# Wv and Wo on GpSimd's DMA queue, and a new order of the preamble, in a two-layer segment-recurrent transformer on one NeuronCore

## Chip, cores and metric

The kernel runs on one core of one Trainium2 chip. The metric is device time in microseconds (us) of one execution, lower is better. Three runs of the kernel before gave 1550.52, 1552.66 and 1554.28 us; the median, 1552.66 us, is the time before. The profiled execution has a span of 1549.6 us with a granted TensorE clock of 0.999.

## What is computed

```
def A(x, mem0, Wq, Wk, Wv, Wo):            # S=2048, Dm=448, H=16, Dh=256, seg=32, M=8
    mem = mem0
    for s in range(64):
        h = concat([mem, x[segment s]])    # 40 rows
        q, k, v = h Wq, h Wk, h Wv         # per head
        p = softmax(mask(q k^T * Dh**-0.5))
        o = sum over heads of (p v) Wo
        mem = o[:8]; outs.append(o[8:])    # the memory rows feed the next segment
def B(x): return (relu(x W_gate) * (x W_up)) W_down     # F=1792
x = x + A(layernorm(x)); x = x + B(layernorm(x))
x = x + A(layernorm(x)); x = x + B(layernorm(x))        # the same weights again
```

Everything is bfloat16 outside PSUM. The 64 segments of one attention layer are a recurrence through `mem`.

## The kernel before

**Folding.** The kernel never forms q, k and v. For each head it forms M = Wk Wq^T and B = Wv Wo once, in a preamble (448x448 each), and keeps them in SBUF for the whole run: `M_sb`/`MT_sb` and `B_sb`/`BT_sb`, where the `T` tiles hold the tail of 64 of the 448 rows. A step then computes G from M and the segment's transposed rows (`GPhase`), the scores S from G, the softmax, the values VO = h B (`Values`, lines 373 to 413), and their weighted sum.

**Steps.** Line 921 runs 70 steps. The first layer's chain C1 takes steps 0 to 63, the second layer's chain C2 runs six steps behind. A step with one chain is `single`, one with two is `dual`. The feed-forward blocks are filled into the steps.

**Preamble (lines 892 to 918).** The weights come in eight parts for Wv and Wo (two heads each) and four parts for Wk and Wq (four heads each):

- `load_vo(j)` (line 174) issues three plain loads: 384 rows of Wv (384 KB), its last 64 rows (64 KB), and 448 KB of Wo. Wv goes to one of two fixed tiles `wvn`, so part j+2 can only be loaded when `turn_B(j)` has read part j. Wo has two buffers, freed by `make_B(j)`.
- `load_kq(i)` (line 171) issues two transposing loads (`load_T`, line 164), each 896 KB: Wk and Wq arrive with the head dimension on the partitions. Each has two buffers, so part i+2 waits for `make_M(i)`.
- `turn_B(j)` transposes a Wv part on TensorE in 16 instructions; `make_B(j)` multiplies in 32; `make_M(i)` multiplies in 32. Their PSUM banks are copied out by ScalarE and VectorE in turn (`copy_out`), those of `make_B(7)` by ScalarE alone.
- `prep_stats`, `prep_rows`, `prep_pe` normalise and transpose 128 rows of x for chain C1. The normalisation takes a reciprocal square root from two GpSimd instructions (lines 253 and 254).
- `first_G[0].quarter(k)` computes a quarter of step 0's G; it needs M from `make_M(k)`.

**What sets the order.** All these loads are issued on SyncE's queue (SP), one after the other. `in_order` (line 117) chains the TensorE instructions, and the loads, in the order in which they are written; a scheduler places the other instructions. The written order of the preamble is: loads of vo 0, vo 1, kq 0; B 0 and B 1; M 0; first x rows; B 2, B 3; M 1; B 4, B 5; quarters 0 and 1; M 2; quarter 2; M 3; quarter 3. Step 0 then has `turn_B(6)`, `turn_B(7)`, `make_B(6)` in its hook `mid` (ahead of the scores) and `make_B(7)` in its hook `soft` (behind the scores, while the softmax runs), and after that the values: `vm` for the memory and a part of the rows, `v` for the others. `part(x, True)` is the tail (with `BT_sb`), `part(x, False)` the body; x = 0 takes the heads of the even B parts, x = 1 those of the odd ones (`place`, line 40).

**GpSimd before.** It clears `memTp`, `mbs`, `PXM`, `PTs` and `maskf` at the start, and issues no loads.

Of the kernel before, what the change touches and what calls it, by code (L numbers as in the profile page):

```python
# [9 lines left out]
BF = mybir.dt.bfloat16  # L10
# [41 lines left out]
def build_kernel(ctx, tc, A_x, A_mem0, A_Wq, A_Wk, A_Wv, A_Wo, B_W_gate, B_W_up, B_W_down, out,  # L52
# [9 lines left out]
    glob = ctx.enter_context(tc.tile_pool(name="glob", bufs=1))  # L62
    R = min(6, ntiles)
    x_ring = glob.tile([P, R, DM], BF)
    nc.sync.dma_start(x_ring[:, 0:2, :], x_dram[0:256].rearrange("(t p) d -> p t d", p=P))

    def xsl(t):
        return x_ring[:, t % R, :]
# [19 lines left out]
    nc.scalar.dma_start(mem_in[:, DM:DMP], mem0[:, 384:448])  # L88
    memTp = []
    for i in range(2):  # L90
        mt = glob.tile([P, NSL, SEG], BF, name=f"memTp{i}")
        nc.gpsimd.memset(mt[:], 0.0)
        memTp.append(mt)
    mbs = []
    for i in range(3):
        m = glob.tile([P, DMP], BF, name=f"mb{i}")
        nc.gpsimd.memset(m[:], 0.0)
        mbs.append(m)
    xns = [glob.tile([P, DMP], BF, name=f"xn{i}") for i in range(2)]
    xds = [glob.tile([P, NCH, 2, 64], BF, name=f"xd{i}") for i in range(2)]  # L100
    n_xn = [0, 0]
    mhalf = glob.tile([P, 1], F32)
    nc.gpsimd.memset(mhalf[:], -0.5)
    p_ln = ctx.enter_context(tc.tile_pool(name="p_ln", bufs=2))

    psum = ctx.enter_context(tc.tile_pool(name="psum", bufs=8, space=bass.MemoryType.PSUM))
# [10 lines left out]
    def in_order(op):  # L117

        eng = op.ins.engine
        if eng in last_of:  # L120
            tc.add_manual_dep(op.ins, last_of[eng],
                              mybir.DependencyInfo(mybir.DependencyClass.NoSync, mybir.DependencyReason.DATA),
                              reason="in_order")
        last_of[eng] = op.ins.name
# [9 lines left out]
    p_pp = ctx.enter_context(tc.tile_pool(name="p_pp", bufs=1))  # L134
    PXM = []
    for i in range(2):
        pp = [p_pp.tile([P, H, SEG], BF, name=f"P{n}{i}") for n in "xm"]
        for q in pp:
            nc.gpsimd.memset(q[:], 0.0)
        PXM.append(pp)  # L140
    PTs = [p_pp.tile([P, 8, P], BF, name=f"PT{i}") for i in range(2)]
    for q in PTs:
        nc.gpsimd.memset(q[:], 0.0)

    bpre = ExitStack()
    bp = bpre.enter_context(tc.tile_pool(name="bpre", bufs=2))
    wvn = [bp.tile([P, NSL, 512], BF, name=f"wvn{i}", bufs=1) for i in range(2)]
    for w in wvn:
        nc.vector.memset(w[HI, 3], 0.0)
    maskf = bp.tile([P, L], F32, bufs=1)  # L150
    nc.gpsimd.memset(maskf[:], 0.0)
    nc.gpsimd.affine_select(
# [4 lines left out]
    nc.vector.memset(maskb[:], 0.0)  # L157
    for half in HALVES:
        nc.vector.tensor_copy(maskb[half], maskf[LO].unsqueeze(1).to_broadcast([64, 8, L]))

    srcs = {n: w.rearrange("d h e -> d (h e)") for n, w in (("k", A_Wk), ("q", A_Wq), ("v", A_Wv))}
    WoF = A_Wo.rearrange("h (t p) d -> p (h t) d", p=P)

    def load_T(n, i):
        t = bp.tile([P, 8, DM], BF, tag=f"w{n}", name=f"w{n}")
        in_order(nc.sync.dma_start_transpose(t[:], srcs[n][:, 1024 * i:1024 * (i + 1)]))  # L166
        return t

    kq, vo = {}, {}

    def load_kq(i):
        kq[i] = load_T("k", i), load_T("q", i)

    def load_vo(j):

        w, cols = wvn[j % 2], slice(512 * j, 512 * j + 512)
        in_order(nc.sync.dma_start(w[:, 0:3, :], srcs["v"][0:384, cols].rearrange("(c p) e -> p c e", p=P)))
        in_order(nc.sync.dma_start(w[LO, 3, :], srcs["v"][384:448, cols]))
        wo = bp.tile([P, 4, DM], BF, tag="wo", name="wo")
        in_order(nc.sync.dma_start(wo[:], WoF[:, 4 * j:4 * (j + 1), :]))  # L180
        vo[j] = w, wo

    flip = [0]

# [18 lines left out]
    def make_M(i):  # L203

        wk, wq = kq.pop(i)
        for hh in range(4):
            o = 896 * ((4 * i + hh) // 2)
            for mt in range(3):
                ps = psum.tile([P, 512], F32, tag="ps")
                product(ps[:, 0:DM], wk, wq, hh, 128 * mt, 128)  # L210
                store_M(M_sb[:, mt, o:o + 896], hh % 2, ps[:, 0:DM])
        for e in range(2):
            ps = psum.tile([P, 512], F32, tag="ps")
            for side in range(2):
                product(ps[64 * side:64 * side + 64, 0:DM], wk, wq, 2 * side + e, 384, 64)
            store_M(MT_sb[:, 896 * i:896 * i + 896], e, ps[:, 0:DM])
# [3 lines left out]
    def turn_B(j):  # L220

        wn = vo[j][0]
        wv = wv_T[j] = bp.tile([P, 4, DM], BF, tag="wv", name="wv")
        for a in range(2):
            tp = psum.tile([P, 2, 512], BF, tag="ps", name="tp")
            for b in range(2):
                for dc in range(NSL):
                    transpose(tp[:, b, 128 * dc:128 * dc + 128],
                              wn[:, dc, 128 * (2 * a + b):128 * (2 * a + b) + 128], ident[:])
            copy_out(wv[:, 2 * a:2 * a + 2, :], tp[:, :, 0:DM])  # L230

    def make_B(j):

        wv, wo = wv_T.pop(j), vo.pop(j)[1]
        for hh in range(2):
            for mt in range(3):
                ps = psum.tile([P, 512], F32, tag="ps")
                product(ps[:, 0:DM], wv, wo, hh, 128 * mt, 128)
                copy_out(B_sb[:, mt, place(2 * j + hh), :], ps[:, 0:DM], j == 7)
        ps = psum.tile([P, 512], F32, tag="ps")  # L240
        for e, half in enumerate(HALVES):
            product(ps[half, 0:DM], wv, wo, e, 384, 64)
        copy_out(BT_sb[:, place(2 * j), :], ps[:, 0:DM], j == 7)
# [320 lines left out]
    def single(g, c, inG, mid, soft, before, late, end, last):  # L564
# [67 lines left out]

        alone = g + 1 < LAG if c is C1 else g + 1 < nsteps and (g + 1 - c.lag) % 4 != 0
        soft()
        if not g:
            vm.both(True)
        vm.both(False)
        if odd:
            vox = prev_vom[0]
            v = ahead[g + 1] = x_values(g + 1) if alone else None  # L640
        else:
            v = ahead.pop(g, None)
            if v is None:
                v = x_values(g)
                v.part(0, False)
                v.part(0, True)
            v.part(1, True)
            vox = v.dst
        prev_vom[0] = VOm
        before()  # L650
# [231 lines left out]
    def none():  # L882
        pass

    def make_two(j):
        turn_B(j)
        turn_B(j + 1)
        for i in (j, j + 1):
            make_B(i)
            load_vo(i + 2)  # L890

    load_vo(0)
    load_vo(1)
    load_kq(0)
    make_two(0)
    load_kq(1)
    make_M(0)
    tps0 = transposed(mem_in, MEM)
    nc.vector.tensor_copy(mem0T[:], tps0[:, :, 0:MEM])
    set_mem0(C1)  # L900
# [2 lines left out]
        prep_rows(C1, t)  # L903
        prep_pe(C1, t)
    make_two(2)
    load_kq(2)
    make_M(1)
    load_kq(3)
    make_two(4)
    if R > 2:  # L910
        in_order(nc.sync.dma_start(x_ring[:, 2:R, :], x_dram[256:R * 128].rearrange("(t p) d -> p t d", p=P)))
    first_G.append(GPhase(0))
    for i in range(2):
        first_G[0].quarter(i)
    make_M(2)
    first_G[0].quarter(2)
    make_M(3)
# [3 lines left out]
    for g in range(nsteps):  # L921
        gb, r = divmod(g, 4)
        if g == LAG:
            set_mem0(C2)
        inG = mid = soft = before = late = end = last = none
        if g == 0:
            def mid():
                turn_B(6)
                turn_B(7)
                make_B(6)  # L930

            def soft():
                make_B(7)
                late_pools()
        elif r == 0:
            def inG():
                fill(0, 1)

            def mid():
                fill(0, 2)  # L940

            def end():
                fill(0, 1)

            def last():
                fill(0, 1)
        elif r == 1:
            def inG():
                prep_stats(C1, gb + 2, recent["G"])

            def mid():
                prep_rows(C1, gb + 2, recent["G"])
                fill(0, 2)

            def before():
                fill(0, 3)
                prep_stats(C2, gb - 1)
                prep_rows(C2, gb - 1)

            def end():  # L960
                prep_pe(C1, gb + 2)
                fill(1, 1)
                prep_pe(C2, gb - 1)

            def last():
                fill(1, 1)
        elif r == 2:
            def inG():
                fill(1, 1)

            def mid():
                fill(1, 1)

            def end():
                fill(1, 1)

            def last():
                fill(1, 1)
        else:
            def mid():  # L980
                fill(1, 1)
                load_x()

            def before():
                fill(1, 1)

            def end():
                fill(1, 1)

            def last():  # L990
                fill(1, 1)
        step(g, inG, mid, soft, before, late, end, last)
        for c in (C1, C2):
            t, j = divmod(g - c.lag, 4)
            if j == 3 and 0 <= t < ntiles:
                f = FFN(c, t)
                f.norm()
                if c is C2 and recent["two"] and g + 1 < nseg and t:
                    f.rows(recent["sum"])
                ffn_q[c.cid].extend(f.pieces())  # L1000
# [54 lines left out]
```

## Time and profile before

| | |
|---|---|
| time, median of 3 | 1552.66 us (1550.52 to 1554.28) |
| profiled span | 1549.6 us |
| TensorE (PE) busy | 1515.6 us, 98% |
| VectorE (DVE), ScalarE (ACT), GpSimd (POOL) busy | 910.5, 625.7, 148.2 us |
| first TensorE instruction | 4.66 us |
| `make_M(0)` begins | 17.39 us |
| `make_M(3)` begins | 57.69 us |
| step 0's first instruction (mask into S) | 65.47 us |
| step 1's first instruction | 83.50 us |

Where PE is busy 98% of the span, only PE's idle time, or PE work that falls away, can shorten it. A line of the timeline gives the start, the length from the first start to the last end, engine, operation, tiles and count, and in brackets the idle time before it and what ended it. SPq is SyncE's sequencer issuing a DMA: its length is the issue, not the transfer. Rows of windows give for each stretch the busy time of each engine, and at the end the granted clock, the DMA engines' busy share (over 1 where packets overlap) and GB/s.

### The profile page before, as it was taken

Reading aid. Unit: us, or ns where it says so; the run is one execution under the profiler, and the core shown is the slowest. Engines: PE = TensorE matmul, PEld = TensorE weight load, DVE = VectorE, ACT = ScalarE, POOL = GpSimd, SP = SyncE. Lnnn points to the kernel's source line nnn. Section 1 sums busy time; section 2 is a strip of 40 time slices with the busy share of each in tenths; the row PEclk is TensorE's granted clock in tenths of the full one; section 3 lists DMA queues with packets and bytes.
Section 4 is the critical chain, followed back from the end, with each engine's and each line's share of the span. In section 5 each row is a group of like instructions: output and inputs, shape, how many; then the busy total and the mean of one; then the engine's idle time right before and its main releaser. Section 6 shows DMA issues by size and latency. Waiting matters only on the chain.

```text
span 1549.6 us, 82294 instructions
## 1 busy us (share of the span) xinstructions
PE 1515.6 (98%) x38579; PEld 1141.7 (74%) x38579; DVE 910.5 (59%) x2085; ACT 625.7 (40%) x1459; POOL 148.2 (10%) x384
## 2 busy tenths in 40 slices
PE   7999999999999999999999999999999999999998
PEld 4566777778777777777778777877777787777775
DVE  5535466665656566556656566565656665656543
ACT  5634344434344343434434343434434343444333
POOL 2001011010101001010001101010100100001000
PEclk9999999999999999999999999999999999999999
DMA  9731000010000000000000101001000000000000
GB/s 238 161 91 44 5 11 15 10 21 12 10 15 16 17 12 19 12 21 6 14 17 12 21 10 21 12 12 14 16 17 12 17 12 14 10 7 14 5 8 9
DMA packets 83636, 39.20 MB, mean 25 GB/s; under 512 B 65752, under 2 KB 82400, under 8 KB 83296
## 3 DMA queue, kind: packets, MB, share of 16 engines
q1 hardware_dynamic: 83264, 33.94, 10.3%
q8 instruction: 301, 4.93, 1.3%
q14 instruction: 39, 0.32, 0.1%
q10 hardware_dynamic: 32, 0.01, 0.0%
HBM read 14.00 MB, written 1.84 MB: 10 GB/s over the span
## 4 chain that ended last, share of the span: by engine, by line
PE 92%; DMA 2%; DVE 2%; SPq 2%; ACT 1%; issue 0%; POOL 0%; POOLq 0%; ACTq 0%
PE gps L127 30%; PE vps L127 28%; PE gate L127 11%; PE AT_ps L127 7%; PE dps L127 6%; PE S_ps L127 5%; PE PT_ps L130 2%; SPq L166 1%; DMA wq<-in_A_Wq_dram 1%; DMA xnT_1184<-xd_91 1%; PE up L127 1%; PE ps L127 1%; PE mps L127 1%; PE tps L130 0%; DVE G L474 0%
## 5 line engine op out<-in xcount | busy, mean ns | idle before, releaser
L127 PE MATMUL gps<-hTr,M_sb 128*128 128x80 bf16 (+1 forms) x11760 | 414.7, 198 | 0.0
L127 PEld LDWEIGHTS <-M_sb 128*128 128x128 bf16 x11760 | 405.3, 99 | 4.4
L474 DVE CAST G<-gps 128x480 bf16<-128x480 f32 (+2 forms) x327 | 194.0, 611 | 222.1 <-PE gps L127 221.4
L474 ACT CAST G<-gps 128x480 bf16<-128x480 f32 (+2 forms) x327 | 165.6, 525 | 350.7 <-PE gps L127 350.7
L127 PEld LDWEIGHTS <-hTr 128*32 128x32 bf16 (+3 forms) x8000 | 177.3, 93 | 142.2 <-issue 42.2
L127 PE MATMUL vps<-B_sb,hTr 128*32 128x448 bf16 x4464 | 234.2, 353 | 0.0
L127 PEld LDWEIGHTS <-Wgu 64*128 64x128 bf16 x6272 | 181.0, 94 | 21.8 <-issue 13.0
L407 ACT CAST VOm<-vps 128x448 bf16<-128x448 f32 x251 | 121.5, 529 | 124.5 <-PE vps L127 124.4
L407 ACT CAST vox<-vps 128x448 bf16<-128x448 f32 x186 | 96.1, 533 | 93.4 <-PE vps L127 89.6
L337 DVE SCALAR_TENSOR_TENSOR hh<-gate,ut 128x256 bf16<-128x256 f32 x224 | 94.7, 423 | 66.4 <-ACT ut L336 66.3
L407 DVE CAST vox<-vps 128x448 bf16<-128x448 f32 x186 | 112.8, 619 | 27.4 <-PE vps L127 25.0
L336 ACT CAST ut<-up 128x256 bf16<-128x256 f32 x224 | 83.8, 374 | 64.8 <-PE up L127 64.8
L127 PE MATMUL up<-xnT_1183,Wgu 64*128 64x128 bf16 x1568 | 104.0, 216 | 0.0
L127 PE MATMUL gate<-xnT_1183,Wgu 64*128 64x128 bf16 x1568 | 103.9, 216 | 0.0
L127 PE MATMUL gate<-xnT_1184,Wgu 64*128 64x128 bf16 x1568 | 99.3, 216 | 2.9 <-DMA xnT_1184<-xd_91 1.8
L127 PE MATMUL up<-xnT_1184,Wgu 64*128 64x128 bf16 x1568 | 99.3, 216 | 0.0
L127 PE MATMUL gps<-hTr,MT_sb 64*128 64x80 bf16 (+1 forms) x3920 | 91.5, 195 | 4.4 <-ACT hTr L693 2.1
L127 PE MATMUL dps<-Wd,hh 128*128 128x448 bf16 x448 | 92.7, 353 | 0.0
L127 PE MATMUL S_ps<-G,hTr 128*8 128x320 bf16 (+3 forms) x2048 | 86.2, 299 | 2.1 <-DVE G L474 1.7
L127 PEld LDWEIGHTS <-MT_sb 64*128 64x128 bf16 x3920 | 76.4, 96 | 15.2 <-issue 7.6
L127 PE MATMUL vps<-B_sb,memTp_80 128*32 128x448 bf16 x1680 | 85.7, 352 | 0.0
L127 PE MATMUL vps<-B_sb,memTp_78 128*32 128x448 bf16 x1680 | 85.7, 352 | 0.0
(163 smaller groups left out, 1607.0 us busy)
## 6 DMA issues: line engine op xcount, KB each, us to landing
wo<-in_A_Wo_dram SPq DMA_DIRECT2D x8, 448.0 KB, 5.4
out_dram<-x_ring SPq DMA_DIRECT2D x16, 112.0 KB, 1.7
Wgu<-in_B_W_gate_dram SPq DMA_DIRECT2D x7, 224.0 KB, 3.5
Wgu<-in_B_W_up_dram SPq DMA_DIRECT2D x7, 224.0 KB, 3.4
Wd<-in_B_W_down_dram SPq DMA_DIRECT2D x7, 224.0 KB, 2.7
wvn_124<-in_A_Wv_dram SPq DMA_DIRECT2D x4, 384.0 KB, 3.7
wvn_125<-in_A_Wv_dram SPq DMA_DIRECT2D x4, 384.0 KB, 6.2
x_ring<-in_A_x_dram SPq DMA_DIRECT2D x10, 112.0 KB, 2.8
```

What stands on the lines that cost most here:

```text
L127: in_order(nc.tensor.matmul(*a, **k))
L130: in_order(nc.tensor.transpose(*a))
L166: in_order(nc.sync.dma_start_transpose(t[:], srcs[n][:, 1024 * i:1024 * (i + 1)]))
L336: recent["ut"] = nc.scalar.copy(ut[:], gu[1][:])
L337: recent["hh"] = nc.vector.scalar_tensor_tensor(out=self.hh[:, f:f + 2, :], in0=gu[0][:], scalar=0.0, in1=ut[:], op0=ALU.max, op1=ALU.mult)
L407: op = self.evac[2 * x + e](self.dst[:, 2 * e + x, :], self.ps[x][e][:, 0:DM])
L474: op = (cp_a, cp_v)[self.side](gp.G[:, self.side, self.t0:self.t0 + self.n, gp.c0:gp.c1, :], self.ps[:, 0:self.n * gp.NP].rearrange("p (m ...
```

## The change

It moves the loads of Wv and Wo to GpSimd's queue, so that Wk and Wq have SyncE's queue to themselves with x; keeps the first transposing load back until the first Wo part has landed; moves the clears on GpSimd behind the first six loads; and gives the preamble and step 0 another order. The core of the diff:

```diff
-    nc.sync.dma_start(x_ring[:, 0:2, :], x_dram[0:256].rearrange("(t p) d -> p t d", p=P))
...
-        nc.gpsimd.memset(mt[:], 0.0)
...
-        nc.gpsimd.memset(m[:], 0.0)
...
-        for q in pp:
-            nc.gpsimd.memset(q[:], 0.0)
...
-    for q in PTs:
-        nc.gpsimd.memset(q[:], 0.0)
...
+    def load_T(n, i):
+        t = bp.tile([P, 8, DM], BF, tag=f"w{n}", name=f"w{n}")
+        dma = nc.sync.dma_start_transpose(t[:], srcs[n][:, 1024 * i:1024 * (i + 1)])
+        if not i and n == "k":
+            tc.add_manual_dep(dma.ins, first_wo[0].ins.name,
+                              mybir.DependencyInfo(mybir.DependencyClass.Sync, mybir.DependencyReason.DATA),
+                              reason="first_wo")
+        in_order(dma)
+        return t
...
+        in_order(nc.gpsimd.dma_start(w[:, 0:3, :], srcs["v"][0:384, cols].rearrange("(c p) e -> p c e", p=P)))
+        in_order(nc.gpsimd.dma_start(w[LO, 3, :], srcs["v"][384:448, cols]))
+        wo = bp.tile([P, 4, DM], BF, tag="wo", name="wo")
+        dma = nc.gpsimd.dma_start(wo[:], WoF[:, 4 * j:4 * (j + 1), :])
+        in_order(dma)
+        first_wo.append(dma)
...
+    load_vo(0)
+    load_vo(1)
+
+    nc.gpsimd.memset(mhalf[:], -0.5)
...
+    for q in memTp + mbs + PXM[0] + PXM[1] + PTs:
+        nc.gpsimd.memset(q[:], 0.0)
...
-    def make_B(j):
+    def make_B(j, between=None):
...
         for hh in range(2):
+            if hh and between:
+                between()
...
-        if not g:
-            vm.both(True)
-        vm.both(False)
+        if g:
+            vm.both(False)
+        else:
+            v = ahead[0] = x_values(0)
+            for x in range(2):
+                vm.part(x, True)
+                v.part(x, True)
+                vm.part(x, False)
+                if not x:
+                    v.part(0, False)
...
-            v.part(1, True)
+            if g:
+                v.part(1, True)
...
     def make_two(j):
-        turn_B(j)
-        turn_B(j + 1)
         for i in (j, j + 1):
-            make_B(i)
-            load_vo(i + 2)
-
-    load_vo(0)
-    load_vo(1)
+            make_B(i, (lambda: turn_B(j + 1)) if i == j else None)
+            if i + 2 < 8:
+                load_vo(i + 2)
+
+    first_G.append(GPhase(0))
     load_kq(0)
+    load_first_x(0, 2)
+    load_kq(1)
+    turn_B(0)
     make_two(0)
-    load_kq(1)
     make_M(0)
+    load_kq(2)
+    turn_B(2)
     tps0 = transposed(mem_in, MEM)
...
     make_two(2)
-    load_kq(2)
     make_M(1)
     load_kq(3)
+    if R > 2:
+        load_first_x(2, R)
+    turn_B(4)
+    first_G[0].quarter(0)
     make_two(4)
-    if R > 2:
-        in_order(nc.sync.dma_start(x_ring[:, 2:R, :], x_dram[256:R * 128].rearrange("(t p) d -> p t d", p=P)))
-    first_G.append(GPhase(0))
-    for i in range(2):
-        first_G[0].quarter(i)
+    first_G[0].quarter(1)
     make_M(2)
...
             def mid():
                 turn_B(6)
-                turn_B(7)
-                make_B(6)
 
             def soft():
-                make_B(7)
+                make_two(6)
                 late_pools()
```

`load_first_x` is a new helper that issues the old x load on SyncE's queue, chained by `in_order`.

More of the change, by code (lines that the diff above doesn't have):

```diff
@@ L90, in build_kernel @@
     for i in range(2):
-        mt = glob.tile([P, NSL, SEG], BF, name=f"memTp{i}")
-        nc.gpsimd.memset(mt[:], 0.0)
-        memTp.append(mt)
+        memTp.append(glob.tile([P, NSL, SEG], BF, name=f"memTp{i}"))
     mbs = []
     for i in range(3):
-        m = glob.tile([P, DMP], BF, name=f"mb{i}")
-        nc.gpsimd.memset(m[:], 0.0)
-        mbs.append(m)
+        mbs.append(glob.tile([P, DMP], BF, name=f"mb{i}"))
     xns = [glob.tile([P, DMP], BF, name=f"xn{i}") for i in range(2)]
@@ L102, in build_kernel @@
     mhalf = glob.tile([P, 1], F32)
-    nc.gpsimd.memset(mhalf[:], -0.5)
     p_ln = ctx.enter_context(tc.tile_pool(name="p_ln", bufs=2))
@@ L136, in build_kernel @@
     for i in range(2):
-        pp = [p_pp.tile([P, H, SEG], BF, name=f"P{n}{i}") for n in "xm"]
-        for q in pp:
-            nc.gpsimd.memset(q[:], 0.0)
-        PXM.append(pp)
+        PXM.append([p_pp.tile([P, H, SEG], BF, name=f"P{n}{i}") for n in "xm"])
     PTs = [p_pp.tile([P, 8, P], BF, name=f"PT{i}") for i in range(2)]
-    for q in PTs:
-        nc.gpsimd.memset(q[:], 0.0)
     bpre = ExitStack()
@@ L149, in build_kernel, with load_kq, load_vo @@
         nc.vector.memset(w[HI, 3], 0.0)
+    srcs = {n: w.rearrange("d h e -> d (h e)") for n, w in (("k", A_Wk), ("q", A_Wq), ("v", A_Wv))}
+    WoF = A_Wo.rearrange("h (t p) d -> p (h t) d", p=P)
+    def load_T(n, i):
[7 more added lines that the diff above has]
+        return t
+    kq, vo = {}, {}
+    first_wo = []
+    def load_kq(i):
+        kq[i] = load_T("k", i), load_T("q", i)
+    def load_vo(j):
+        w, cols = wvn[j % 2], slice(512 * j, 512 * j + 512)
+        in_order(nc.gpsimd.dma_start(w[:, 0:3, :], srcs["v"][0:384, cols].rearrange("(c p) e -> p c e", p=P)))
[4 more added lines that the diff above has]
+        first_wo.append(dma)
+        vo[j] = w, wo
+    load_vo(0)
+    load_vo(1)
+    nc.gpsimd.memset(mhalf[:], -0.5)
     maskf = bp.tile([P, L], F32, bufs=1)
@@ L159, in build_kernel @@
         nc.vector.tensor_copy(maskb[half], maskf[LO].unsqueeze(1).to_broadcast([64, 8, L]))
[L161 to L181, printed above, removed]
+    for q in memTp + mbs + PXM[0] + PXM[1] + PTs:
+        nc.gpsimd.memset(q[:], 0.0)
     flip = [0]
@@ L883, in none, with load_first_x @@
         pass
+    def load_first_x(lo, hi):
+        in_order(nc.sync.dma_start(x_ring[:, lo:hi, :], x_dram[lo * 128:hi * 128].rearrange("(t p) d -> p t d", p=P)))
     def make_two(j):
-        turn_B(j)
-        turn_B(j + 1)
         for i in (j, j + 1):
-            make_B(i)
-            load_vo(i + 2)
-    load_vo(0)
-    load_vo(1)
+            make_B(i, (lambda: turn_B(j + 1)) if i == j else None)
+            if i + 2 < 8:
+                load_vo(i + 2)
+    first_G.append(GPhase(0))
     load_kq(0)
+    load_first_x(0, 2)
+    load_kq(1)
+    turn_B(0)
     make_two(0)
-    load_kq(1)
     make_M(0)
+    load_kq(2)
+    turn_B(2)
     tps0 = transposed(mem_in, MEM)
```

## The prediction

> **What bounds the kernel now.** I read the page's slices first.
>
> ```profile
> PE   7999999999999999999999999999999999999998
> ...
> DMA  9731000010000000000000101001000000000000
> GB/s 238 161 91 44 5 11 15 10 21 12 10 15 16 17 12 19 12 21 6 14 17 12 21 10 21 12 12 14 16 17 12 17 12 14 10 7 14 5 8 9
> ```
>
> A slice is 38.7 us. TensorE is full everywhere but at the start, and the DMA engines are busy only there. Everything that the change touches lies ahead of step 1 (83.50 us); from there the steps are the same instructions in the same written order. So I ask only when step 1 starts; the rest, 1469 us, shifts with it. Next, the chain of waits for the first 84 us, in order of time (start, length, what):
>
> ```profile
> 4.70 6.63 SPq L166
> 11.37 5.88 DMA wq<-in_A_Wq_dram
> ...
> 27.37 6.22 DMA wq<-in_A_Wq_dram
> ...
> 42.34 7.45 DMA wq<-in_A_Wq_dram
> ...
> 75.00 0.44 ACT BT_sb L188
> ```
>
> The chain runs over SyncE's queue and the landings of Wq, not over TensorE, until M 2 starts at 49.93; then over TensorE. Then TensorE's timeline, to see what that costs in idle time:
>
> ```profile
> 4.66 0.50 PE L130 MATMUL tp<-ident,wvn_124 128*128 128x128 bf16 x3 [4.66 <-DMA wvn_124<-in_A_Wv_dram]
> 6.32 1.54 PE L130 MATMUL tp<-ident,wvn_124 128*128 128x128 bf16 x13 [1.16 <-DMA wvn_124<-in_A_Wv_dram]
> 10.65 6.47 PE L127 MATMUL ps<-wo,wv 128*128 128x448 bf16 x32
> 17.39 5.58 PE L127 MATMUL ps<-wq,wk 128*128 128x448 bf16 x32 [0.28 <-DMA wq<-in_A_Wq_dram]
> 33.73 5.58 PE L127 MATMUL ps<-wq,wk 128*128 128x448 bf16 x32 [2.58 <-DMA wq<-in_A_Wq_dram]
> 49.93 5.58 PE L127 MATMUL ps<-wq,wk 128*128 128x448 bf16 x32 [0.20 <-DMA wq<-in_A_Wq_dram]
> 75.49 0.36 PE L127 MATMUL vps<-BT_sb,memTp_78 64*32 64x448 bf16 x2 [0.69 <-ACT BT_sb L188]
> ```
>
> M 0, M 1 and M 2 each start when their Wq lands, but only M 1 lost much: 2.58 us. The last view is the windows over the DMA engines, whose last two columns are busy share and GB/s:
>
> ```profile
> 24.50:26.00 1.50, 1.50 (x22) 1.23 (x20) 1.11 (x4) 1.36 (x3) 0.00 (x0) 1.00 1.78 47
> 46.00:48.50 2.50, 2.50 (x77) 1.75 (x75) 1.42 (x3) 1.09 (x3) 0.00 (x0) 1.00 1.28 290
> 52.50:53.50 1.00, 1.00 (x7) 0.49 (x5) 1.00 (x3) 0.56 (x2) 0.00 (x0) 1.00 0.06 7
> 57.00:64.50 7.50, 6.90 (x88) 3.81 (x85) 5.17 (x12) 4.15 (x11) 0.00 (x0) 1.00 0.97 298
> ```
>
> A transposing load streams at 290 GB/s, plain loads at 298, but between a plain load and a transposing one, or two transposing ones, stand gaps of 1 to 2 us in which almost nothing moves (7 and 47 GB/s). Ordinary loads on a second queue could fill these.
>
> [...]
>
> **The change part by part.**
>
> *First loads from GpSimd.* The trace of before has no load issued by GpSimd. SyncE's issues take 0.46 to 0.59 us, my lower bound. [...] I take 1 us[...]. GpSimd's first load can begin after the identity's two instructions, about 1.2 us. The first Wo is the third: issue begins at 3.2, [...] it has landed: 6.3 us (5.3 and 8.3 at the bounds; before it landed at 2.36 + 5.2 = 7.6). An estimate.
>
> *`turn_B(0)` and B 0, B 1.* The first Wv half lands about as before, near 5 us; `turn_B(1)` no longer stands ahead of B 0. So B 0 starts near 7.5 instead of 10.65, and B 1 ends near 14 instead of 17.1. This pays nothing by itself: M 0 waits for Wq.
>
> *The new wait.* The first transposing load waits for the first Wo: 6.3 instead of 4.70 us. Behind it on SyncE's queue stand Wq 0, x and kq 1; TensorE's M 0 waits for them. Without other traffic a pair takes as long as the last pair of before, from issue at 47.17 to landing at 51.09 + 6.5 = 57.6: 10.4 us. Wq 0 then lands at 16.7, against 17.25.
>
> *Competition.* GpSimd's queue has no order against it: vo 2 and vo 3 are let through by `turn_B` and `make_B` from about 7.5 to 14 us, before Wq 0 has landed. Count bytes: until then must move vo 0, 1 and 2 (0.918 MB each), Wv of vo 3 (0.459) and the pair (1.835 MB), 5.05 MB; at 298 GB/s from 2 us that is 16.9, to 18.9 us, and 0.6 us from the data's end to landing (wq 3: 57.0 to 57.6) gives 19.5. Some of vo 3 comes later: without it 18.0. I take 18.6: M 0 at 18.6 rather than 17.39, 1.2 us lost. Bounds: 16.7 (gaps take all) and 23.2 (first Wo at 8.3, plus 10.4, plus 1.35 MB at 298 GB/s wholly added).
>
> *From M 0 to M 3.* Between the two starts TensorE does the same work as before, only reordered: 57.69 - 17.39 = 40.30, of which waits for Wq are 2.58 + 0.20. These vanish: kq 1 follows kq 0 and x directly; at most 10.4 us and 3 us of competition after kq 0 it has landed, near M 0 + 12, and M 1 needs it at M 0 + 13.7 (33.73 - 2.58 - 17.39). kq 2 waits for M 0 and kq 3 for M 1; each has over 17 us until its product. The later Wv and Wo are loaded one round ahead. The waits for M's copies at quarter 2 (0.26 + 0.41) stay. Gain 2.8 us.
>
> *x rows.* They now come behind Wq 0: issued near M 0 - 2, landed near M 0 + 1.3. Statistics, rows and copies are 2 x (0.6 + 0.15 + 0.39 + 0.17) = 2.6 us of VectorE and two rounds of GpSimd (0.2 + 0.57), beside M 0's copies, of which VectorE has about 4.5 us. TensorE needs them after M 0 and `turn_B(2)`, at M 0 + 6.4. It nearly fits; I charge 0.2 us (0 to 2). If the scheduler placed them on GpSimd behind a waiting load, it would be the upper end.
>
> *Clears.* About 7 us of GpSimd, moved behind six issues. First needed: `memTp` near 25 us, the others in step 0. Cost nothing, hidden by the B and M products.
>
> *Step 0.* B 6 moves behind the scores. The last quarter's copies to G (65.57 + 0.45) lie under `turn_B(6)`'s 0.9 us; the softmax, 71.47 to 74.6, has more to hide under than before. The values begin with x = 0, which needs no part of B 7, so the 0.69 us for `BT_sb` vanish. The last copies of `vm` then stand closer to the weighted sum; 0.1 us back. Gain 0.6 us.
>
> Sum: +1.2 - 2.8 + 0.2 - 0.6 = -2.0 us, so 1550.6; I say 1550.5 us.
>
> **Rivals.**
>
> *A. Small gain, as above:* 1550.5, chance 0.45. What is won at M 1 is partly paid at M 0.
>
> *B. The gaps take the plain loads:* Wq 0 lands at 16.7, or at 15.7 with the quicker issue (5.3). Then -0.7 to -1.7 at M 0, -2.8, -0.6: -4.1 to -5.1, about 1548. For it: each transposing pair leaves over 2 us of gaps in 10.4. Against: the gaps may belong to the transposing itself, and start-up has the most plain traffic. Chance 0.40.
>
> *C. GpSimd's queue costs more than it frees:* slow issue and competition bring M 0 to 23.2 (+5.8), x another 1.5: +5.8 + 1.5 - 2.8 - 0.6 = +3.9, 1556.5. For it: nothing in the trace prices GpSimd's issue, and transposing loads now share engines all the way. Against: the first six loads would have to take 2 us each. Chance 0.15.
>
> **How the numbers follow.** The likeliest is A. 0.2% is 3.1 us: B is faster (0.40), A within (0.45), C slower (0.15). For 8 in 10 I take all of A, most of B down to 1545.5 (its 1548 less 2.5, for the runs' own spread of up to 2.1 us about their median), and C to 1555.5, leaving its tail out.
>
> **What would show it.** Right: no wait for Wq ahead of M 1 to M 3, and none of 0.69 us for `BT_sb` in step 0; B 1 done near 14 us and then TensorE idle until Wq 0, near 18.6; the windows' gaps narrower; step 1 at about 81.5. Wrong: Wq 0 before 17 us or after 21; issues on GpSimd of 2 us; a wait of over 1 us at the x transposes; a Wv or Wo part that comes late because GpSimd's queue stands waiting; or steps from 1 on that no longer take the same time.

## The result, and the profile after

The kernel after takes 1562.48 us (median of 4 runs, 1560.05 to 1564.86), the kernel before beside it 1551.59 us (1548.61 to 1554.28): a ratio of 1.0071, 95% interval 1.0042 to 1.0099. It is slower by about 11 us. The forecast was 1550.5 us, and the range ended at 1555.5. The profiled execution of the kernel after is the slowest of its four (1564.86 us), so its stages show somewhat more than the 11 us.

The page's slices of the kernel after (40 slices of 39.1 us):

```profile
PE   4999999999999999999999999999999999999998
...
GB/s 206 190 58 74 5 11 15 12 16 10 14 17 12 20 11 21 12 9 17 14 18 12 19 12 21 12 9 17 14 19 12 16 12 14 7 10 14 5 8 9
```

Only the start differs: TensorE's first slice went from 7 tenths to 4. The steps are what they were: from step 1's start to the end of the span it is 1465.3 us, before 1466.1. So the loss lies ahead of step 1, in these stages (starts in us, from one profiled execution of each kernel):

| | before | after | change of the stage that ends here |
|---|---|---|---|
| B 0 begins | 10.65 | 7.82 | |
| B 1 done | 17.1 | 16.4 | |
| M 0 begins | 17.39 | 27.41 | +10.0 |
| M 1 begins | 33.73 | 48.91 | +5.2 |
| M 3 begins | 57.69 | 72.53 | -0.3 |
| step 1 begins | 83.50 | 97.51 | -0.8 |

The chain of waits of the kernel after, in order of time, has in its first 28 us:

```profile
3.21 4.57 DMA wo<-in_A_Wo_dram
...
7.80 4.78 SPq L144
...
12.64 14.64 DMA wq<-in_A_Wq_dram
```

The new wait for the first Wo is there (it lands at 7.78 us), but the length to see is the last: Wq 0 lands 14.6 us after its issue begins; before it took 5.9. TensorE's timeline shows what that does:

```profile
13.47 2.95 PE L121 MATMUL ps<-wo,wv 128*128 128x448 bf16 x16 [0.37 <-DVE wv L193]
27.41 7.48 PE L121 MATMUL ps<-wq,wk 128*128 128x448 bf16 x32 [11.00 <-DMA wq<-in_A_Wq_dram]
...
39.32 0.61 PE L124 MATMUL tps<-ident,xn_83 128*128 128x128 bf16 x4 [2.08 <-DVE xn_83 L272]
...
48.91 5.59 PE L121 MATMUL ps<-wq,wk 128*128 128x448 bf16 x32
...
89.18 0.38 PE L121 MATMUL vps<-BT_sb,memTp_77 64*32 64x448 bf16 x8
```

The 2.58 us ahead of M 1 and the 0.69 us for `BT_sb` are gone, as the change meant; one wait of 11.00 us took their place. M 0 itself takes 7.48 us instead of 5.58, and a second wait, 2.08 us for the x rows, is new. Part of that one is a price of the new issuer. In the chain of waits, a Wv part that GpSimd has to issue (0.61 us in all) stands between the two GpSimd instructions that the second x row needs:

```profile
37.55 0.12 POOL wvn_111 L162
...
38.18 0.60 POOL rstd L259
```

Who had the DMA engines while M 0 waited? The view of the DMA engines for 20 to 24 us of the kernel after (packets, MB, share of 16 engines); q0 is GpSimd's queue, q1 SyncE's:

```profile
DMA packets 564, 0.92 MB, mean 229 GB/s; under 512 B 358, under 2 KB 375, under 8 KB 564
q0 software_dynamic: 245, 0.84, 81.1%
q1 hardware_dynamic: 319, 0.08, 10.7%
```

Nine tenths of the bytes are Wv and Wo of parts 2 and 3, which TensorE needs only behind M 0. Between 16 and 18 us, when SyncE's queue had the engines alone, it moved 265 GB/s; here it gets 0.08 MB in 4 us, 20 GB/s. By the packet records, 6851 of the 7168 packets of Wk 0 and Wq 0 had started by 20.0 us; the rest trickled, 60 to 100 each us, until 24.2. The landing comes 3.1 us behind the last of them, at 27.27.

The windows of the kernel after explain M 0's own length; the last three columns are granted clock, DMA share and GB/s:

```profile
22.00:24.00 2.00, 0.00 (x0) 0.00 (x0) 0.00 (x0) 0.00 (x0) 0.00 (x0) 0.50 0.97 243
28.00:30.00 2.00, 2.00 (x7) 0.78 (x6) 1.15 (x2) 0.68 (x2) 0.00 (x0) 0.50 0.91 207
```

TensorE, idle since 16.4 us, was granted half its clock from about 21 us, and still had it when M 0 began; full speed came back near 31.3 us.

The +5.2 us from M 0 to M 1 can be summed from the timeline. Before, that stage took 16.34 us, of which 2.58 were the wait, so 13.76 of work. After: 13.76 + 1.90 (M 0 begins at half clock) + 0.66 + 2.08 (the two waits at the x rows) + 2.48 (B 2, `turn_B(3)` and B 3 take 9.19 us from 39.72 to 48.91, 5.2 us of it at half clock, where the same instructions at full clock take 6.71, from 25.18 to 31.89 in the kernel that puts all loads back on SyncE's queue) = 20.88 of the 21.50 measured.

### The profile page after: what moved, and what is told of

Its sections match the earlier page's. It is cut to its first block, busy times and chain, and to the rows that moved or that the text cites. A ratio compares the mean times of both kernels' runs of the same rounds, so it can differ in the third digit from the quotient of the medians.

```text
span 1562.8 us, 82310 instructions
## 1 busy us (share of the span) xinstructions
PE 1519.1 (97%) x38579; PEld 1141.7 (73%) x38579; DVE 914.2 (59%) x2085; ACT 625.7 (40%) x1459; POOL 165.1 (11%) x408
## 4 chain that ended last, share of the span: by engine, by line
PE 93%; DVE 2%; DMA 2%; ACT 1%; POOL 0%; issue 0%; SPq 0%; POOLq 0%; ACTq 0%
PE gps L121 30%; PE vps L121 28%; PE gate L121 11%; PE AT_ps L121 7%; PE dps L121 6%; PE S_ps L121 5%; PE ps L121 3%; PE PT_ps L124 2%; PE up L121 1%; DMA wq<-in_A_Wq_dram 1%; DMA xnT_1184<-xd_85 1%; PE mps L121 1%; PE tps L124 0%; PE tp L124 0%; SPq L144 0%
```

## The experiments

The theory: what fails is the transposing load beside plain loads of another queue. The rivals: the new order of TensorE's work; GpSimd's queue being slow by itself; x behind Wq; the wait for the first Wo; any two queues together.

**Keep vo 2 back.** The kernel after, with one more wait:

```diff
+        if j == 2:
+            tc.add_manual_dep(wv.ins, last_T["q", 0].ins.name, ...)   # vo 2's first load waits for Wq 0
```

> The changed kernel, with one wait more: the first load of the third Wv part on GpSimd's queue waits until Wq 0 has landed. Theory 'competition' (Wq 0 landed at 27.3 us because GpSimd's queue took the DMA engines from 13.4 us on): Wq 0 lands near 18 us, 10.4 us after the first transposing load is issued at 7.8; M 0 starts near 18.3 instead of 27.4, TensorE's clock stays at 1.0, and the whole takes 1552 to 1555 us, about as before, since the third and fourth Wv/Wo parts then stand in the way of kq 1. Rival 'own queue' (what is late is the pair itself, behind the wait for the first Wo, with x and Wk 1 queued behind it): Wq 0 still lands after 24 us and the time stays at 1560 or more.

Measured: 1573.55 us (1572.18 to 1577.77), ratio 1.0155 (1.0138 to 1.0172). TensorE's timeline of this kernel:

```profile
18.68 5.58 PE L122 MATMUL ps<-wq,wk 128*128 128x448 bf16 x32 [2.11 <-DMA wq<-in_A_Wq_dram]
...
39.88 8.42 PE L122 MATMUL ps<-wq,wk 128*128 128x448 bf16 x32 [4.28 <-DMA wq<-in_A_Wq_dram]
```

With vo 2 and vo 3 held back, M 0 starts at 18.68, 8.7 us earlier than in the kernel after: the loads of GpSimd's queue are what Wq 0 waited for. But the total, expected at 1552 to 1555, missed by some 19 us: the held loads now met the later pairs of transposing loads (waits of 4.28, 4.89 and 3.79 us ahead of M 1, M 2 and M 3, each at the reduced clock; step 1 at 105.66).

**The new order on the old queue, and ScalarE's queue in place of GpSimd's.** In the first, all loads go back to SyncE's queue in the order of before, x ahead and no wait for Wo; TensorE's order and the clears stay as after. In the second only the issuer of Wv and Wo changes.

```diff
-        in_order(nc.gpsimd.dma_start(w[:, 0:3, :], ...))
+        in_order(nc.sync.dma_start(w[:, 0:3, :], ...))      # second kernel: nc.scalar.dma_start
...
-    load_kq(1)
     turn_B(0)
     make_two(0)
+    load_kq(1)
```

> The changed kernel with its order of TensorE's work, but all loads back on SyncE's queue in the order of before, no wait for the first Wo, x first. If the loss comes from GpSimd's queue alone: M 0 near 17.0, M 1 near 33.5, no wait for B 7 in step 0, step 1 at 82.5 to 83, so 0.5 to 1 us under before: 1550.8. If the new order of TensorE's work is itself part of the loss (quarter 0 early, turn_B between the halves, B 6 behind the scores): above before, 1555 or more.

> The changed kernel with the Wv and Wo loads issued by ScalarE instead of GpSimd; everything else is kept. On SyncE's queue the plain loads of before moved in packets of about 1 KB, on GpSimd's in packets of 3.4 KB, beside 256 B of a transposing load. Theory 'packets' ([...] the larger packets starve the transposing load): [...] Wq 0 lands near 21 to 23 us. Theory 'any second queue' (a transposing load's completion waits until the other queue is empty): Wq 0 lands when the last Wo part let through has landed, 26 us or later.

Measured on SyncE's queue: 1549.46 us (1547.88 to 1551.73), ratio 0.9991 (0.9983 to 1.0). M 0 starts at 18.03, M 1 at 33.86, step 1 at 84.14. So the new order of TensorE's work costs nothing in the total; the loss belongs to the loads: their queue, the place of x, and the wait for the first Wo. The ratio is the lowest of all, but with its interval reaching 1.0 this kernel can't be told from the kernel before. Step 1, expected at 82.5 to 83, comes later because M 1 waited and then ran in part at half clock (5.58 us at full clock):

```profile
33.86 7.26 PE L122 MATMUL ps<-wq,wk 128*128 128x448 bf16 x32 [1.97 <-DMA wq<-in_A_Wq_dram]
```

On ScalarE's queue, one execution: 1555.8 us, M 0 at 22.32 after a wait of 5.88, step 1 at 89.26. A wait of that kind appears without GpSimd as issuer. Wq 0 landed within the 21 to 23 us that the theory of packets gave. This doesn't decide between the theories, since in the next experiment M 0 started at 22.37 in one execution with GpSimd's larger packets.

**x ahead of everything.** The kernel after with x issued first on SyncE's queue, as before; one execution, and later seven more of the same kernel.

```diff
+    nc.sync.dma_start(x_ring[:, 0:2, :], x_dram[0:256].rearrange("(t p) d -> p t d", p=P))
...
-    load_first_x(0, 2)
```

> The changed kernel with the first x load back at the head of SyncE's queue. Theory: of the 21.5 us from M 0 to M 1 (16.3 before), 2.7 us are TensorE's waits for the x rows and some 2 us the low clock that follows them. M 0 stays at 26 to 28 us; M 0 to M 1 falls to 15.5 to 17.5 us (1.9 us of low clock behind the wait for Wq stay), and the time to about 1557. Rival: the rows are not to blame, VectorE is late with M 0's copies and the clock is low for the long wait alone: M 0 to M 1 stays above 19.5 us.

> The kernel of e4 (x first, else the changed kernel), timed in rounds. If its single time of 1552.4 holds, moving one load of 224 KB accounts for about 10 of the 11 us: 1551 to 1553.5. If the early landing of Wq 0 (22.2 instead of 27.3) was chance: 1556 to 1560.

Measured: the single execution gave 1552.36 us with M 0 at 22.37; the seven gave 1561.26 us (1553.37 to 1570.19), ratio 1.0073 (1.0043 to 1.0104), with M 0 at 27.14 in their profile. The good first time was chance. The stage from M 0 to M 1 did shorten, to 16.64 and 15.96 us with no wait for x rows, so x behind Wq is a cost of the stage. It could not be resolved in the total, because the same kernel varies by 17 us: how hard the two queues collide differs from one execution to the next, as the two profiles show, where the kernel before stays within about 7 us.

**No wait for the first Wo.** The kernel with x first, without the wait of the first transposing load; then the same with Wv and Wo on ScalarE's queue.

```diff
-        if not i and n == "k":
-            tc.add_manual_dep(dma.ins, first_wo[0].ins.name, ..., reason="first_wo")
```

> The changed kernel with x back at the head of SyncE's queue and without the wait of the first transposing load for the first Wo. Theory 'competition': what delays Wq 0 is overlap with plain loads on the other queue, so an early pair still crawls while the first six loads move (until about 9 us) and then needs its own 8 us: Wq 0 near 17 to 19, ahead of most of the third and fourth parts; M 0 at 18 to 19.5 instead of 22.4, step 1 at 83 to 84.5, 1548 to 1550.5 us. Rival 'the wait for the first Wo is worth its cost': the first pair's plain loads are held up by the transposing ones, B 0 starts 2 us or more later than 8.6, Wq 0 lands no earlier than 22, and the time is 1552 or more.

> The kernel of e5 (x first, no wait for the first Wo, else the changed kernel) with Wv and Wo issued by ScalarE instead of GpSimd. In e5 the DMA engines moved 60 to 160 GB/s in most of the first 16 us, while a plain load on GpSimd's queue and a transposing one were both under way. Theory 'any two streams': the same collapse with ScalarE's queue; TensorE starts after 10 us, time 1565 or more. Theory 'GpSimd's queue' (its packets of up to 4 KB beside 256 B): no collapse, over 220 GB/s from 3 to 16 us, TensorE starts before 7 us, M 0 before 20 us, 1549 to 1553 us.

Measured with GpSimd's queue: 1578.49 us (1571.86 to 1591.63), ratio 1.0195 (1.0141 to 1.0249); with ScalarE's: 1568.83 us (1564.62 to 1571.78), ratio 1.0118 (1.0098 to 1.0138). TensorE's first instruction comes at 15.18 and 10.62 us. The windows of the kernel with GpSimd's queue, the last column GB/s:

```profile
4.00:6.00 2.00, 0.00 (x0) 0.00 (x0) 1.45 (x6) 0.00 (x0) 2.00 (x3) 1.00 1.38 121
6.00:8.00 2.00, 0.00 (x0) 0.00 (x0) 0.00 (x0) 0.00 (x0) 2.00 (x10) 1.00 1.14 58
8.00:10.00 2.00, 0.00 (x0) 0.00 (x0) 0.00 (x0) 0.00 (x0) 2.00 (x6) 1.00 1.53 131
```

The engines are busy (shares above 1), and move 58 to 131 GB/s, where a transposing load alone streamed at 290 in the kernel before. So the engines don't merely share: here, with both kinds of load under way, the bytes per second fall by half and more (58 to 131 against 290). I call this the collapse. The expectation of 1548 to 1550.5 us missed; its rival came true, and the wait for the first Wo is worth some 17 us (1578.49 without it, 1561.26 with it). GpSimd's queue is not needed for the collapse. The view of the DMA engines for 8 to 12 us of the kernel with ScalarE's queue (q10):

```profile
q1 hardware_dynamic: 1465, 0.38, 86.1%
q10 hardware_dynamic: 261, 0.24, 41.8%
```

From the shares: 0.861 x 16 engines x 4 us over 1465 packets is 38 ns for one packet of a transposing load. Streaming alone in the kernel before (46 to 48.5 us, 2834 packets at a share of 127.5%) one takes 18 ns. A plain packet of about 0.9 KB takes 102 ns, where it takes 46 beside plain loads alone (the experiment with two queues of plain loads). Here both kinds get longer. But the two kinds don't always collapse. From 16 to 18 us of this same kernel both queues have packets all the time, and the engines move 310 GB/s:

```profile
q10 hardware_dynamic: 501, 0.44, 71.1%
q1 hardware_dynamic: 708, 0.18, 42.4%
```

The total of this kernel holds a cost of ScalarE's own too: ahead of B 3's products TensorE waits 4.85 us for a copy of ScalarE, which now also issues loads.

**Fill the wait.** The kernel after with 64 added products of 320 columns between B 1 and M 0, whose results are not used, so that TensorE isn't idle.

```diff
+    for i in range(64):
+        matmul(fill_ps[:, 0:8 * L], ident[:], maskb[:], start=(i == 0), stop=(i == 63))
     make_M(0)
```

> The changed kernel with 64 matmuls of 320 columns on constants put into TensorE's wait ahead of M 0 (8.5 us of work for the 11 us wait; their result is not used). Theory 'clock': M 0 takes 7.5 instead of 5.6 us because the clock fell to 0.5 in the wait; kept busy, TensorE has clock 1.0 at M 0, M 0 takes 5.6 to 6 us, and the time falls by 1.5 to 3 us, to about 1560. Rival 'copies': M 0 is slow because VectorE is held by the x rows; then M 0 stays at 7.3 us or more at clock 1.0 and the time at 1562.

Measured: 1565.45 us (1563.15 and 1567.75), ratio 1.01 (1.0077 to 1.0124); the 1560 expected missed. In its profile the granted clock is 1.00 from 15 to 37 us, where the kernel after has 0.50 from 21.05 to 31.29, so the reduced clock there does come from the idle stretch. M 0's products took 3.56 and 2.18 us, 5.74 together, near the 5.58 of full clock, but with a stop between them:

```profile
34.33 2.18 PE L121 MATMUL ps<-wq,wk 128*128 128x448 bf16 x14 [2.49 <-DVE M_sb L193]
```

In VectorE's queue of this kernel all the work on the two x rows (30.29 to 33.74 us) stands ahead of M 0's copies, and x lands behind Wq 0; in the kernel after only one instruction of it does. So the numbers are those of the rival 'copies', but the stop came with this edit, which moved VectorE's order as well; the total doesn't show what the clock alone is worth.

**Step 0's order alone,** in the kernel before.

```diff
             def mid():
                 turn_B(6)
-                turn_B(7)
-                make_B(6)
             def soft():
+                make_B(6, lambda: turn_B(7))
                 make_B(7)
```

and the new order of the values, as in the change.

> The kernel before with the new order of step 0 alone (B 6 behind the scores, turn_B(7) between its halves, values of x = 0 first). From M 3's start to step 1 the changed kernel took 24.98 us and the kernel before 25.81. Theory: this is the order alone; step 1 starts 0.8 us earlier, 82.7 instead of 83.5, and the time falls by 0.5 to 1 us (ratio 0.9994). Rival: the order only gains where TensorE came late to step 0; no difference (within 0.3 us).

Measured: 1549.98 us (1548.08 to 1551.57), ratio 0.9999 (0.999 to 1.0008). From M 3's start to step 1 it is 25.00 us instead of 25.81. The stage gains the 0.8 us; the total can't resolve it. The profile shows something else, though. The loads of the preamble are those of the kernel before, yet M 1 begins without a wait:

```profile
31.84 5.60 PE L127 MATMUL ps<-wq,wk 128*128 128x448 bf16 x32
```

It comes 13.70 us after M 0, where the profile of before has 16.34, and step 1 comes at 80.45. So the wait of 2.58 us, from which most of the forecast's gain was to come, isn't in every execution of these loads.

**The overlap alone, in the kernel before.** Only vo 2 and vo 3 go to GpSimd's queue; everything else is as before.

```diff
+        eng = nc.gpsimd if j in (2, 3) else nc.sync
-        in_order(nc.sync.dma_start(w[:, 0:3, :], ...))
+        in_order(eng.dma_start(w[:, 0:3, :], ...))
```

> The kernel before with only the third and fourth Wv/Wo parts (2 of 8) issued on GpSimd's queue; no other edit. Theory 'collision': let through by turn_B and make_B from about 9 to 17 us, they meet Wq 0 and the second pair on SyncE's queue; Wq 0 lands after 19 us or Wq 1 after 36 us (17.3 and 33.6 before), with under 200 GB/s in that stretch, and the time is 1554 to 1562. Rival 'it takes the whole rearrangement' (the wait for the first Wo, the late x, the new order): two parts change little, Wq 1 lands by 33 us since SyncE's queue is shorter by six issues, and the time is 1547 to 1551.

Measured: 1554.49 us (1551.07 to 1560.07), ratio 1.0022 (1.0008 to 1.0036). While Wq 1 and vo 3 are both under way, the windows show:

```profile
24.00:26.00 2.00, 2.00 (x26) 1.17 (x25) 1.93 (x10) 1.54 (x5) 0.00 (x0) 1.00 1.76 140
26.00:28.00 2.00, 2.00 (x35) 1.82 (x33) 1.77 (x6) 1.79 (x5) 0.61 (x3) 1.00 0.85 86
28.00:30.00 2.00, 2.00 (x13) 0.90 (x11) 1.54 (x3) 1.74 (x3) 0.00 (x0) 1.00 1.36 144
```

From 30 to 32 us it is 63 GB/s, although no more packets of vo 3 start there. SyncE's issue of Wq 1 takes 9.63 us (4.19 before). Two parts moved to the other queue are enough for the collapse and for part of the loss, though TensorE's order, x, the clears and the first wait are those of before.

**Two queues of plain loads only.** The kernel before, with vo 1 issued by ScalarE beside vo 0 on SyncE's queue, and the first transposing load held until Wo 1 has landed.

```diff
+        eng = nc.scalar if j == 1 else nc.sync
...
+        if not i and n == "k":
+            tc.add_manual_dep(dma.ins, wo_dma[1].ins.name, ..., reason="plain_pair")
```

> The kernel before with one second queue of plain loads, but never beside a transposing load: Wv 1 and Wo 1 are issued by ScalarE while SyncE issues Wv 0, Wo 0 and x, and the first transposing load waits until Wo 1 has landed. Theory (only a transposing load beside plain loads collapses): the engines move 250 GB/s or more between 2.5 and 8 us, TensorE starts before 6 us, B 0 starts by 10.7 us, M 0 comes 1 to 4 us later than before because the transposing loads are held to about 8 or 9 us (18.5 to 21.5), and the time is 1551 to 1555 us. Rival (any two busy queues collapse): less than 200 GB/s between 2.5 and 9 us, Wo 1 lands after 11 us, B 0 later than 12 us, M 0 after 22 us, the time 1556 us or more.

Measured: 1552.51 us (1550.17 to 1555.46), ratio 1.0011 (1.0003 to 1.0018). TensorE starts at 4.75 us, B 0 at 10.48, M 0 at 19.73. The DMA view of this kernel for 2.5 to 8 us:

```profile
DMA packets 1828, 1.66 MB, mean 302 GB/s; under 512 B 105, under 2 KB 1828, under 8 KB 1828
q1 hardware_dynamic: 1090, 0.98, 59.2%
q10 hardware_dynamic: 738, 0.68, 38.6%
```

302 GB/s, and 46 ns a packet on ScalarE's queue (0.386 x 16 x 5.5 us over 738). Two busy queues of plain loads did no harm here. With the kernel on ScalarE's queue above, this puts the collapse on the transposing load beside plain ones; the rival of any two queues falls. No run had GpSimd's queue busy beside plain loads of another alone.

**Strict turns.** The kernel after, with waits both ways so that GpSimd's loads and transposing loads are not under way together; only the end of vo 1, until about 10 us, still overlaps the first pair.

```diff
+HOLD = {2: 0, 4: 1, 6: 3}          # the first load of vo j waits for Wq HOLD[j]
...
+        if n == "k" and i < 3:     # Wk 0, 1, 2 wait for Wo 0, 3, 5
+            tc.add_manual_dep(dma.ins, first_wo[(0, 3, 5)[i]].ins.name, ...)
```

> The kernel after with the two queues taking strict turns: Wv and Wo stay on GpSimd's queue, but vo 2 waits for Wq 0, vo 4 for Wq 1, vo 6 for Wq 3, and Wk 1 waits for Wo 3, Wk 2 for Wo 5, so that a plain load from GpSimd and a transposing load are never under way together. Theory (the overlap is the loss): each pair of transposing loads lands about 10.4 us after its issue, the two queue issues of a pair take about 4.8 us each, M 0 near 18.7, M 1 at 36 to 39, step 1 at 89 to 93 because the turns add landing latencies, 1556 to 1560 us, and the executions lie within 3 us of each other. Rival (GpSimd's queue is slow by itself): pairs are quick, but GpSimd's parts take over 6 us each from issue to landing with nothing beside them, M 1 after 42, 1562 us or more. Second rival (the transposing loads themselves are disturbed by something else than the plain loads): pairs take over 13 us even alone.

Measured: 1562.35 us (1560.54 to 1564.7), ratio 1.0071 (1.0056 to 1.0086). TensorE's timeline:

```profile
18.30 7.26 PE L122 MATMUL ps<-wq,wk 128*128 128x448 bf16 x32 [1.86 <-DMA wq<-in_A_Wq_dram]
...
38.83 7.26 PE L122 MATMUL ps<-wq,wk 128*128 128x448 bf16 x32 [4.03 <-DMA wq<-in_A_Wq_dram]
```

M 0 starts at 18.30, as expected, and M 1 at 38.83 (36 to 39 expected), and a pair lands 10.9 and 9.6 us after its issue: with hardly any plain load beside it, or none, a pair is as quick as the last one of the kernel before (10.4). The executions lie within 4.2 us, expected 3. Step 1 comes at 94.25, past the 89 to 93 expected, and the total misses the expected 1556 to 1560. The excess is in the turns: two parts take 10.5 us from the first issue to the last landing (18.75 to 29.2), the pair behind them 9.6; a round of 20.1 us then stands against some 14 us of TensorE's work, and the waits let the clock fall again. Part of this is the rival's: with nothing but x's end beside them GpSimd's parts still took 10.5 us, where the first two parts took 8.9 in the run with two queues of plain loads (1.24 to 10.12). So taking turns between the two queues loses as much here as colliding (1562.35 and 1562.48 us). One queue, on which a load is issued without waiting for the landing of the one ahead (before, Wk 3 is issued at 47.17 and Wq 2 lands at 49.79), beat both.

## Why the prediction was wrong

Step by step, in its own order.

- **First loads from GpSimd.** Issues take 0.54 to 1.00 us, and the 1 us assumed is the longest of them. Wo lands at 7.78 us rather than 6.3, still inside the upper bound of 8.3: 4.57 us after its issue began, where the forecast had 3.1 (6.3 less 3.2). That length was the author's estimate; no trace of before had a load of GpSimd's to show it.
- **B 0 and B 1.** B 0 starts at 7.82, forecast 7.5. B 1 ends at 16.4 rather than 14: the sum had left out `turn_B(1)`, which now stands between the halves of B 0 (10.02 to 11.29), and TensorE waited 0.37 us for a copy of VectorE, which stood behind the casts of the mask (4.47 us, see the last section). Neither was on the path.
- **The new wait.** The pair starts at 7.80 rather than 6.3, a miss of 1.5 us, and alone it would take about what was said: 10.4 us forecast, 10.9 in the run with turns.
- **Competition: this step failed.** It was sized at +1.2 us with an upper bound of +5.8 and measured +10.0. It counted all bytes up to Wq 0's landing and moved them at 298 GB/s, as if two queues shared a fixed sum. The count was near: 5.05 MB, where 5.22 moved in the kernel after from 2 us to 24.2, when the pair's last packet starts.

```profile
DMA packets 8230, 5.22 MB, mean 235 GB/s; under 512 B 7400, under 2 KB 7458, under 8 KB 8230
```

What was wrong is the rate, 235 GB/s instead of 298, so that the data end at 24.2 rather than 18.9 us, and the time from there to the landing, 3.1 us instead of 0.6. Together they are the 7.8 us from the 19.5 of the count to 27.27. The rest of the miss is the 0.9 us that the forecast of 18.6 had taken off for a part of vo 3. The sum isn't fixed: with a transposing load beside plain loads the engines moved 58 to 195 GB/s from 4 to 12 us of the two kernels without the first wait. And in the kernel after the share isn't even: with 96% of the pair's packets started, the rest got 20 GB/s while loads that nobody waited for got 210. In the trace a packet of the pair has 256 B and one of GpSimd's queue 3.4 KB in the mean, and of the bytes from 20 to 24 us the pair has 9%. The large packets don't cover all: with ScalarE's of about 0.9 KB the loss is there as well (107 to 195 GB/s from 4 to 12 us), and the packets themselves get longer (38 ns instead of 18, 102 instead of 46).
- **The gaps.** The idea behind the change, that another queue can use them, rests on a misread line. The window from 24.50 to 26.00 us in the prediction has 47 GB/s, but at a share of 1.78: its 278 packets are under way and slow, 154 ns each (1.782 x 16 x 1.5 us over 278) instead of 18. Only the window with a share of 0.06 is idle. The slow stretch is where vo 3 ends and Wk 1 begins, on one queue: plain and transposing packets meet there before the change too, for 1 to 2 us. That it is the same effect as the collapse is not shown.
- **From M 0 to M 3.** The waits for Wq, 2.58 and 0.20 us, vanished as forecast, and M 1 to M 3 took 23.62 us (before 23.96). In part this is no merit of the change, since Wq 1 had all of M 0's delay to land in, and the 2.58 us are not in every execution of the loads of before. And a term was missing: the waits let TensorE's clock fall to 0.50, which cost 1.9 us in M 0 and some 2.5 in B 2 and B 3.
- **x rows.** Sized at 0.2 us, with 2 at most; measured 0.66 + 2.08 = 2.74. The prediction named GpSimd's queue as what could bring the upper end, and an issue of GpSimd was indeed in the way. With x first the stage has no such wait.
- **Clears.** Not on the path, as said, but VectorE's casts of the mask took 4.47 us beside them, before 0.64: see the last section.
- **Step 0.** Forecast -0.6, measured -0.8.

Rival C (GpSimd's queue costs more than it frees, 0.15) had the right sign and the right place, at M 0 and the x rows. Of its two reasons, the slow issue was wrong (0.54 to 1.00 us), and the competition was right but too small; its 1556.5 us was too low by 6. The likeliest case and rival B both rested on the idea that gaps in the transposing stream can be filled from another queue. No order tried here with a second queue was faster than the one queue of the kernel before.

Why a transposing load and a plain one slow each other, packet by packet, is not settled by these runs; nor why they don't always, and why the collision is so uneven from one execution to the next.

## What to carry to other kernels

When a profile shows few bytes in a stream of transposing loads, read the busy share beside them: few bytes at a share over 1 (here 47 GB/s at 1.78) are packets under way and slow, not room for more. Don't plan to fill such a gap with plain loads from another queue before one such overlap is measured, by moving a single load: here two parts moved left 63 to 144 GB/s from 24 to 32 us. In a chain of loads that a matrix product waits for, one queue in the order of need also protected the urgent load here from the loads that nobody waited for yet (the chain has 5.88 us of Wq 0 before, 14.64 after); with two queues that order was lost, and explicit waits between the queues gave it back only at the price of a landing each time (a round of 20.1 us against some 14 us of TensorE's work). And a forecast that adds a wait ahead of TensorE should add the slower clock that can stand behind it (M 0 took 7.48 us behind 11.00 us of wait, 5.58 before). A wait that one profile shows ahead of a product should be found in a second execution before its removal is booked as a gain.

## What the runs showed of the hardware that was not expected

- A transposing load beside plain loads of another queue: 58 to 131 GB/s (GpSimd's queue, 4 to 10 us of that run) and 107 to 195 GB/s (ScalarE's, 4 to 12 us), against 290 for a transposing load alone and 302 for two queues of plain loads. It isn't always so: 310 from 16 to 18 us with ScalarE's queue.
- One kernel with this overlap, the one with x first, ran from 1553.37 to 1570.19 us.
- In the wait for Wq 0 TensorE's granted clock fell to 0.50 some 2.1 us (two queues of plain loads) and 4.6 us (the kernel after) after TensorE fell idle, and came back 3.1 and 3.9 us after M 0 began there, 6.5 us on ScalarE's queue; with the idle stretch filled it stayed at full speed. In the kernel after it fell once more at 38.12 us, 0.9 us into the wait of 2.08 us for the x rows. The clock records have these stretches at 0.50: 34.28 to 37.69 us on SyncE's queue (3.41 us), 38.12 to 44.94 in the kernel after (6.82), 21.05 to 31.29 there (10.24). The length of the wait alone didn't decide: behind 1.97 us M 1 took 7.26 us on SyncE's queue, behind 2.11 us M 0 took 5.58 in the run that kept vo 2 back, and the 3.06 us still idle ahead of M 0 in the run that filled the wait left the clock at 1.00. What else decides is not shown.
- VectorE's casts of the mask took 4.47 us where the clears moved on GpSimd ran beside them, and 0.64 and 0.83 us where no clear did. The casts in the kernel after, in the kernel before, and in the kernel with x first and no wait:

```profile
7.75 4.47 DVE L182 CAST maskb<-maskf 64x320 bf16<-64x320 f32 x2
...
12.80 0.64 DVE L159 CAST maskb<-maskf 64x320 bf16<-64x320 f32 x2
...
19.82 0.83 DVE L179 CAST maskb<-maskf 64x320 bf16<-64x320 f32 x2
```

In the first the casts end at 12.22, half a us behind the last clear, which ends at 11.70. In the third the clears stand in the same place, and are over at 11.7 us, before the casts start; in the second they are over at 6.6. The run with turns is as the first: casts from 7.77 to 12.26, the last clear over at 11.74. So in both of these profiles where clears were running when the casts started, the casts ended 0.5 us behind the last clear; what held them until then is not shown. It cost nothing here because M 0 was waiting for Wq anyway.
